# Dividing attention outputs by their sums in twelve pairs instead of eight, with the factors turned in front of the products with V

## The chip, the cores and the metric

The kernel runs on one core of one Trainium2 chip. Its metric is the device time of one execution in microseconds. The engines are TensorE (PE, with weight loads as PEld), VectorE (DVE), ScalarE (ACT), GpSimd (POOL) and SyncE (SP), which only issues transfers. Each works through its own queue in the order in which the program was written to it, and waits where an instruction needs another engine's result or a buffer that is still in use.

## The reference

Attention with a causal window of 128 and four sink columns, then a feed-forward layer with a cosine, then a mixture of experts with one expert a token. The change touches the division by the row sum in the attention.

```python
def _attn_ref(q, k, v, n_sink, window):          # 4 batches, 8 heads, S = 768, D = 64
    scores = scale * np.matmul(q, k.transpose(0, 1, 3, 2))
    keep = is_sink | in_window                    # 4 sink columns, window 128
    scores = np.where(keep, scores, -1000000000.0)
    scores = scores - np.max(scores, axis=-1, keepdims=True)
    a = np.exp(scores)
    a = a / (np.sum(a, axis=-1, keepdims=True) + 1e-09)
    return np.matmul(a, v)
x = attn_out.transpose(0, 2, 1, 3).reshape(3072, 512)
h = x @ w_in                                      # 512 x 2048
x = (h * np.cos(h)) @ w_out                       # 2048 x 512
...
out[mask] = gate_w[mask, None] * (np.maximum(x[mask] @ w1[e], 0.0) @ w2[e])   # 8 experts, top 1
```

Since the division is by one number a row, it can be made on P = exp(scores) before the product with V, or on the product. Everything is kept in float32 by a high part and a rest: a tile named ..._h holds the rounded value and ..._l what it leaves, and a product is formed of three.

## The kernel before

The sequence of a batch is worked on in two halves of 384 rows (three blocks of 128). There are eight such half-sequences, hb 0 to 7, with four pairs of heads each: pairs 0 to 3 are hb 0, pairs 4 to 7 hb 1, pairs 8 to 11 hb 2, and so on to pair 31. While the attention of hb runs, the same program runs the feed-forward layer on tile hb−1, whose products are hp (with w_in) and y (with w_out). In the first third it also converts the weights from their loaded form into high part and rest (cv_in, cv_out, cv_s, cv_a, wi_l, wo_l). The mixture of experts comes last.

The steps of one pair, in the order of the code: q and k are turned on TensorE (pq L447, pk L469) and split; scores ps for each block and head, from which VectorE takes the masked values and their row maxima mx (L548); exp with the row sums sm on ScalarE (L564); P is turned block by block (pt L588, L589) and split into pT_h (ScalarE) and pT_l (VectorE); the sink columns are copied to pc, turned to pz (L613) and split into sp; and the product with V is added up in po. po is the transposed output of two heads, 128 x 384: a column is a row of the sequence.

The division has two forms, chosen by `whole`.

- `whole` (hb 2 and later before the change): P itself is multiplied by 1/sum. For each of the three blocks VectorE adds 1e-9 to two sums and takes the reciprocal (L571), and in hb 2 POOL multiplies the two heads' P (helper line L142, called at L576); from hb 3 on VectorE does. Behind po ScalarE copies it to xT_h (L644) and VectorE subtracts to xT_l (L645, recorded under the helper line L148).
- not `whole` (hb 0 and 1 before): one addition and one reciprocal for all six columns of sm (L598). POOL spreads the factors to 128 columns, one copy a block (L601), TensorE turns these three (pf), ScalarE copies pf to xs (L651), VectorE multiplies po by it (L652), ScalarE rounds to xT_h (L653) and POOL subtracts to xT_l (L654).

From hb 3 on the products with V use another, stacked form; its division is the `whole` one. In hb 0 and 1 the odd pairs are "extra": they have tiles of their own for P (pb_x) and their loads.

All of ps, pt, pz, po, pf, pq and pk come from one rotation of three banks of PSUM (the extra pairs of hb 0 use the three banks of y instead), so a tile has to wait until the one that stood three places earlier in that rotation has been read. A scheduler takes the instructions as the code yields them, with weights for the steps, and sets the order of each engine's queue from its own costs; that order is then fixed.

Of the kernel before, what the change touches and what calls it, by code (L numbers as in the profile page):

```python
# [11 lines left out]
F32 = DT.float32  # L12
# [4 lines left out]
AF = mybir.ActivationFunctionType  # L17
# [3 lines left out]
P = 128  # L21
# [27 lines left out]
EX = 1  # L49
# [5 lines left out]
NPOOL = 3  # L55
# [6 lines left out]
def kernel(  # L62
# [23 lines left out]
    HALF = S // 2  # L86
    NQ = HALF // P
# [14 lines left out]
    PE, ACT, DVE, POOL, SP = nc.tensor, nc.scalar, nc.vector, nc.gpsimd, nc.sync  # L102
# [21 lines left out]
    def ps_a(name):  # L124
        return ps_rot(0, "a", name)
# [4 lines left out]
    def ps_y(i, name):  # L130
        return psum.tile([P, 512], F32, tag=f"y{i}", name=name, bufs=1)
# [3 lines left out]
    def mm(o, l, r, start, stop):  # L135
        PE.matmul(o, l, r, start=start, stop=stop)  # L136
# [14 lines left out]
    ident = const.tile([P, P], F32, name="ident")  # L151
# [76 lines left out]
    pb_x = [wpool.tile([P, DM], F32, name=f"pb_x{f}", tag=f"wi_h{f}") for f in range(NE1, NF)]  # L228
# [6 lines left out]
    apool = att.enter_context(tc.tile_pool(name="apool", bufs=1, side="right"))  # L235
# [84 lines left out]
    def steps(hb):  # L320
        return STEPS_0 if hb <= 1 else STEPS_1
# [82 lines left out]
    def attn_front(hb, pr):  # L404
# [3 lines left out]
        h0 = 2 * pr  # L408
        extra = hb <= EX and pr % 2 == 1

        whole = hb > EX
        n_ps = [0]

        def psb(name):
            if hb > 0 or not extra:
                return ps_a(name)
            n_ps[0] += 1
            return ps_y(n_ps[0] % NQ, name)
# [29 lines left out]
        stack = hb >= STACK  # L448
# [118 lines left out]
        def rest():  # L567
            xh, xl = xT[hb]
            for t in range(NQ if whole else 0):
                ts(DVE, sm[:, 2 * t:2 * t + 2], sm[:, 2 * t:2 * t + 2], 1e-9, ALU.add)  # L570
                DVE.reciprocal(sm[:, 2 * t:2 * t + 2], sm[:, 2 * t:2 * t + 2])  # L571
                for j in range(2):
                    c0, c1, _ = cols(t)
                    i = 2 * t + j
                    if hb < NPOOL:
                        ts(POOL, Pb[t][j][:, c0:c1], Pb[t][j][:, c0:c1], sm[:, i:i + 1], ALU.mult, 0.0, ALU.add)  # L576
                    else:
                        ts(DVE, Pb[t][j][:, c0:c1], Pb[t][j][:, c0:c1], sm[:, i:i + 1], ALU.mult)
            yield steps(hb)[3]
            pT_h = apool.tile([P, 2, NQ * 256], F32R, name="pT_h")  # L580
            pT_l = apool.tile([P, 2, NQ * 256], F32R, name="pT_l")
            for t in range(NQ):
                pt = psb("pt").rearrange("p (j x) -> p j x", j=2)
                first = half == 0 and t == 0
                s0 = P if first else 0
                for j in range(2):
                    if not first:
                        PE.transpose(pt[:, j, 0:P], Pb[t][j][:, 0:P], ident)  # L588
                    PE.transpose(pt[:, j, P:2 * P], Pb[t][j][:, SEG:W3], ident)  # L589
                oh = pT_h[:, :, t * 256 + s0:(t + 1) * 256]  # L590
                ol = pT_l[:, :, t * 256 + s0:(t + 1) * 256]
                ACT.activation(out=oh, in_=pt[:, :, s0:256], func=AF.Copy)
                tt(DVE, ol, pt[:, :, s0:256], oh.bitcast(F32), ALU.subtract)
                yield steps(hb)[4]
            if not whole:

                ts(DVE, sm, sm, 1e-9, ALU.add)
                DVE.reciprocal(sm, sm)  # L598
                rb = [pb_x[t + NQ * (pr % 2)][:, 3 * P:4 * P] for t in range(NQ)]
                for t in range(NQ):  # L600
                    POOL.tensor_copy(rb[t].rearrange("p (j d) -> p j d", d=D),  # L601
                                     sm[:, 2 * t:2 * t + 2].unsqueeze(2).to_broadcast([P, 2, D]))
            t0 = 2 if half == 0 else 0
            pc = apool.tile([P, NQ, 2, NS], F32, name="pc")
            if extra:
                for t in range(t0, NQ):
                    for j in range(2):
                        POOL.tensor_copy(pc[:, t, j], Pb[t][j][:, P:SEG])
            else:
                (POOL if hb < NPOOL else DVE).tensor_copy(pc[:, t0:], Pt[:, t0:, :, P:SEG])  # L610
            pz = psb("pz")
            for t in range(t0, NQ):
                PE.transpose(pz[0:2 * NS, t * P:(t + 1) * P], pc[:, t].rearrange("p j s -> p (j s)"), ident)  # L613
            sh, sl = sp[0:2 * NS], sp[2 * NS:4 * NS]
            if half == 0 and pr == 0:

                POOL.memset(sp[0:4 * NS, 0:t0 * P].bitcast(F32), 0.0)
            ACT.activation(out=sh[:, t0 * P:], in_=pz[0:2 * NS, t0 * P:HALF], func=AF.Copy)
            tt(DVE, sl[:, t0 * P:], pz[0:2 * NS, t0 * P:HALF], sh[:, t0 * P:].bitcast(F32), ALU.subtract)
            yield steps(hb)[5]  # L620
            def band(blk):

                own = blk if half == 0 else blk - 1
                ta, tb = max(own, 0), min(own + 1, NQ - 1)
                c0 = ta * P
                c1 = (tb + 1) * P
                m0 = own * 256 + P if own >= 0 else 0
                return c0, c1, m0, m0 + (c1 - c0)

            if not stack:  # L630

                po = psb("po")
                mm(po[:, 0:HALF], vs[:, 0:2 * D], sp, True, False)
                mm(po[:, 0:HALF], vs[:, 2 * D:4 * D], sp, False, False)
                for j in range(2):
                    for blk in range(nblk):
                        c0, c1, m0, m1 = band(blk)
                        vh, vl = [vp[:, blk, (o + j) * D:(o + j + 2) * D] for o in (0, 3)]
                        mm(po[:, c0:c1], vh, pT_h[:, j, m0:m1], False, False)
                        mm(po[:, c0:c1], vh, pT_l[:, j, m0:m1], False, False)  # L640
                        mm(po[:, c0:c1], vl, pT_h[:, j, m0:m1], False, j == 1 and blk == nblk - 1)
                        yield steps(hb)[6]
                if whole:
                    ACT.activation(out=xh[:, pr, :], in_=po[:, 0:HALF], func=AF.Copy)  # L644
                    tt(DVE, xl[:, pr, :], po[:, 0:HALF], xh[:, pr, :].bitcast(F32), ALU.subtract)  # L645
                else:
                    pf = psb("pf")
                    for t in range(NQ):
                        mm(pf[:, t * P:(t + 1) * P], rb[t], ident, True, True)
                    xs = apool.tile([P, HALF], F32, name="xs")  # L650
                    ACT.activation(out=xs, in_=pf[:, 0:HALF], func=AF.Copy)  # L651
                    tt(DVE, xs, po[:, 0:HALF], xs, ALU.mult)  # L652
                    ACT.activation(out=xh[:, pr, :], in_=xs, func=AF.Copy)  # L653
                    tt(POOL, xl[:, pr, :], xs, xh[:, pr, :].bitcast(F32), ALU.subtract)  # L654
            if stack:
                xs = apool.tile([P, HALF], F32, name="xs")
            for j in range(2 if stack else 0):

                po = psb("po")
                mm(po[:, 0:HALF], vs[:, j * 2 * D:(j + 1) * 2 * D], sp, True, False)  # L660
                for blk in range(nblk):
                    c0, c1, m0, m1 = band(blk)
                    mm(po[:, c0:c1], vp[:, blk, 3 * j * D:(3 * j + 2) * D], pT_h[:, j, m0:m1], False, False)
                    mm(po[:, c0:c1], vp[:, blk, (j + 1) * D:(j + 3) * D], pT_l[:, j, m0:m1], False, blk == nblk - 1)
                    yield steps(hb)[6]
                r = slice(j * D, (j + 1) * D)
                ACT.activation(out=xs[r], in_=po[r, 0:HALF], func=AF.Copy)
                tt(DVE, xs[r], po[(1 - j) * D:(2 - j) * D, 0:HALF], xs[r], ALU.add)
            if stack:
                ACT.activation(out=xh[:, pr, :], in_=xs, func=AF.Copy)  # L670
                tt(POOL, xl[:, pr, :], xs, xh[:, pr, :].bitcast(F32), ALU.subtract)
            for dst, x_ in ((xg_h, xh), (xg_l, xl)):
                SP.dma_start(out=x_[:, pr, :].bitcast(F32), in_=dst[half, b * H + h0:b * H + h0 + 2].rearrange("j d q -> (j d) q"), cond=bad_r > 0, cond_hint=False)
            yield steps(hb)[7]
# [376 lines left out]
    for hb in range(1, NTILE):  # L1051
# [8 lines left out]
        whole = attn_weight(hb) * ATT_STEPS[hb % 2] * (S_FIRST if hb == 1 else 1.0)  # L1060
# [31 lines left out]
    for nm in ("xT_h", "xT_l"):  # L1092
        t = xpool.tile([P, KD, 256], F32R, name="m_" + nm, tag=nm)
# [344 lines left out]
```

## Time and profile before

| | us |
|---|---|
| median of three runs | 1224.01 (1221.92 to 1226.13) |
| profiled execution, its own time | 1220.77 |
| its span | 1218.9 |
| TensorE busy | 1140.5 (94%) |
| VectorE busy | 799.0 (66%) |
| ScalarE busy | 698.7 (57%) |
| POOL busy | 341.0 (28%) |

The mean granted clock of TensorE is 0.974 of full speed over the span; in the second of forty slices of the span it is 0.7, in the third and the sixth 0.8. The share of TensorE grows along the program: 32.47 of the first 50 us, 41.33 of the next, and from 260 us on nearly all. A row of the profile names line, engine and operation, then what is written and read; a wait is given as the idle time in front of an instruction and what ended it.

### The profile page before, as it was taken

To read this page: it belongs to the slowest core of one execution; us is meant where nothing else is said; L and a number is where in the kernel's file an instruction comes from. 1 tells how busy PE (TensorE), PEld (TensorE's weight loads), DVE (VectorE), ACT (ScalarE), POOL (GpSimd) and SP (SyncE) were. 2 spreads that over 40 slices of the span, in tenths; PEclk is the share of its full clock that TensorE was granted. 3 is DMA by queue.
4 is the path that set the end of the run, shared out by engine and by line. 5 is a ranking of instruction groups with operands and counts; after the bars stand their busy time and mean duration, and the time that the engine had idled before them with its cause. 6 is when DMAs were issued, how large, how long until landed. Compare 5 with 4: busy or idle time off the path is not lost. (4 is left out here: it accounts for less than half of the span.)

```text
span 1218.9 us, 21841 instructions
## 1 busy us (share of the span) xinstructions
PE 1140.5 (94%) x6688; PEld 1007.7 (83%) x6688; DVE 799.0 (66%) x2293; ACT 698.7 (57%) x1451; POOL 341.0 (28%) x396
## 2 busy tenths in 40 slices
PE   5888897899999999999999999999999999899995
PEld 4667776788878888988889888999889988789984
DVE  7886798968887888788878878464672223722220
ACT  4667576678767777877688876333422224622221
POOL 2534545542223223322232222231212112112110
PEclk9789989999999999999999999999999999999998
DMA  5553255534332343334224322261424113212110
GB/s 142 138 164 121 84 170 162 163 95 98 81 95 69 84 103 97 82 77 104 77 78 116 96 70 78 92 246 53 104 92 162 37 44 133 88 45 63 37 37 24
DMA packets 141338, 118.87 MB, mean 98 GB/s; under 512 B 98415, under 2 KB 107631, under 8 KB 141168
## 3 DMA queue, kind: packets, MB, share of 16 engines
q1 hardware_dynamic: 136848, 103.29, 30.5%
q0 software_dynamic: 4320, 13.65, 3.5%
q8 instruction: 66, 1.08, 0.4%
q14 instruction: 104, 0.85, 0.2%
HBM read 151.32 MB, written 19.67 MB: 140 GB/s over the span
## 5 line engine op out<-in xcount | busy, mean ns | idle before, releaser
L148 POOL TENSOR_TENSOR g_l<-ch,g_h 128x384 fp32r<-128x384 f32 x128 | 131.8, 1030 | 413.3 <-ACT g_h L760 379.7
L136 PE MATMUL hp<-xT_h,wi_h 128*128 128x384 f32 x512 | 183.1, 358 | 1.5 <-DVE ch L148 1.5
L136 PE MATMUL hp<-xT_l,wi_h 128*128 128x384 f32 x512 | 174.5, 341 | 0.0
L136 PE MATMUL hp<-xT_h,wi_l 128*128 128x384 f32 x512 | 174.2, 340 | 0.0
L688 PE MATMUL y<-wo,g_h 128*128 128x512 f32 x384 | 160.4, 418 | 0.4 <-ACT y_part L778 0.4
L688 PE MATMUL y<-wo_l,g_h 128*128 128x512 f32 x384 | 158.5, 413 | 0.0
L688 PE MATMUL y<-wo,g_l 128*128 128x512 f32 x384 | 156.0, 407 | 0.2 <-POOL g_l L148 0.2
L136 PE MATMUL m_y<-wi_h,hT 128*128 128x512 f32 x416 | 132.7, 394 | 1.6 <-ACT hT L1182 0.7
L145 DVE SCALAR_TENSOR_TENSOR hT<-m_h,hT 128x256 fp32r<-128x256 f32 x88 | 37.4, 425 | 145.5 <-ACTq L1346 97.1
L750 ACT ACTIVATE ch<-ch,cols 128x384 f32<-128x384 f32 x128 | 78.9, 616 | 89.2 <-DVE ch L145 88.0
L136 PEld LDWEIGHTS hp<-xT_h,wi_h 128*128 128x128 f32 x512 | 97.9, 191 | 6.7 <-DVE ch L148 1.8
L136 PEld LDWEIGHTS hp<-xT_l,wi_h 128*128 128x128 f32 x512 | 97.9, 191 | 3.8 <-issue 0.2
L142 DVE TENSOR_SCALAR ch<-hp 128x384 int32<-128x384 f32 x128 | 71.1, 555 | 43.5 <-PE hp L136 26.7
L136 PEld LDWEIGHTS hp<-xT_h,wi_l 128*128 128x128 f32 x512 | 97.2, 190 | 0.4
L136 PEld LDWEIGHTS m_y<-wi_h,hT 128*128 128x128 f32 x416 | 78.0, 188 | 18.7 <-ACT hT L1182 1.5
L760 ACT ACTIVATE g_h<-ch 128x384 fp32r<-128x384 f32 x128 | 66.4, 519 | 42.1 <-DVE ch L148 32.3
L564 ACT ACTIVATE Pb<-Pb,mx 128x272 f32<-128x272 f32 (+1 forms) x168 | 82.7, 493 | 13.5 <-DVE mx L548 12.9
L148 DVE TENSOR_TENSOR ch<-ch,hp 128x384 f32<-128x384 f32 x128 | 70.2, 550 | 27.8 <-ACT ch L750 26.2
L1163 ACT ACTIVATE hT<-m_h 128x256 fp32r<-128x256 f32 x88 | 33.7, 383 | 90.2 <-PE m_h L136 84.4
L688 PEld LDWEIGHTS y<-wo,g_l 128*128 128x128 f32 x384 | 73.6, 192 | 14.3 <-POOL g_l L148 0.6
L1197 POOL DMA_INDIRECT out_dram<-m_ot,m_ids x26 | 26.7, 1027 | 198.5 <-ACT m_ot L1194 147.9
L136 PE MATMUL ps<-kT_hl,qT_h 64*128 64x272 f32 (+3 forms) x264 | 59.0, 348 | 24.2 <-DVE mx L548 10.3
(307 smaller groups left out, 2958.0 us busy)
## 6 DMA issues: line engine op xcount, KB each, us to landing
rw<-in_moe_w_dram SPq DMA_DIRECT2D x112, 512.0 KB
wo_l<-wl_scr SPq DMA_DIRECT2D x122, 256.0 KB
cv_in<-in_moe_w_in_dram SPq DMA_DIRECT2D x16, 512.0 KB
cv_out<-in_moe_w_out_dram SPq DMA_DIRECT2D x16, 512.0 KB
y_scr<-yt SPq DMA_DIRECT2D x24, 256.5 KB
xT_h<-xg_h SPq DMA_DIRECT2D x32, 192.0 KB
xT_l<-xg_l SPq DMA_DIRECT2D x32, 192.0 KB
qn<-in_q_dram SPq DMA_DIRECT2D x56, 96.0 KB
```

Of the source, the lines that this page charges most:

```text
L136: PE.matmul(o, l, r, start=start, stop=stop)
L142: e.tensor_scalar(out=o, in0=i, scalar1=s1, scalar2=s2, op0=op0, op1=op1)
L145: e.scalar_tensor_tensor(out=o, in0=i0, scalar=s, in1=i1, op0=op0, op1=op1)
L148: e.tensor_tensor(out=o, in0=a, in1=b, op=op)
L564: ACT.activation(out=Pb[t][j][:, c0:c1], in_=Pb[t][j][:, c0:c1], func=AF.Exp, scale=-1.0, bias=mx[:, i:i + 1], accum_out=sm[:, i:i + 1])
L688: i = PE.matmul(o, l, r, start=start, stop=stop)
L750: ACT.activation(out=ch, in_=ch, func=AF.Sin, scale=TWO_PI, bias=half_pi)
L760: ACT.activation(out=gh, in_=ch, func=AF.Copy)
L1163: ACT.activation(out=hT_h[f], in_=hp, func=AF.Relu)
L1197: POOL.indirect_dma_start(out=out[:, :], out_offset=bass.IndirectOffsetOnAxis(ap=m_ids[T % 4][:, h:h + 1], axis=0), in_=m_ot[h], in_offset ...
```

## The change

`whole` now begins at hb 3 instead of hb 2, so that pairs 8 to 11 divide the output too. In all twelve pairs the spread factors rb no longer lie in spare columns of pb_x but in the first 128 columns of the first head's P of each block, which the copies may overwrite once TensorE has turned them. The matmuls pf and ScalarE's copy to xs are written in front of pz and po instead of behind po.

```diff
-        whole = hb > EX
+        whole = hb >= NPOOL
...
                 yield steps(hb)[4]
+            xs = None if whole and not stack else apool.tile([P, HALF], F32, name="xs")
             if not whole:
 
                 ts(DVE, sm, sm, 1e-9, ALU.add)
                 DVE.reciprocal(sm, sm)
-                rb = [pb_x[t + NQ * (pr % 2)][:, 3 * P:4 * P] for t in range(NQ)]
+                rb = [Pb[t][0][:, 0:P] for t in range(NQ)]
                 for t in range(NQ):
                     POOL.tensor_copy(rb[t].rearrange("p (j d) -> p j d", d=D),
                                      sm[:, 2 * t:2 * t + 2].unsqueeze(2).to_broadcast([P, 2, D]))
+                pf = psb("pf")
+                for t in range(NQ):
+                    mm(pf[:, t * P:(t + 1) * P], rb[t], ident, True, True)
+                ACT.activation(out=xs, in_=pf[:, 0:HALF], func=AF.Copy)
...
                 else:
-                    pf = psb("pf")
-                    for t in range(NQ):
-                        mm(pf[:, t * P:(t + 1) * P], rb[t], ident, True, True)
-                    xs = apool.tile([P, HALF], F32, name="xs")
-                    ACT.activation(out=xs, in_=pf[:, 0:HALF], func=AF.Copy)
                     tt(DVE, xs, po[:, 0:HALF], xs, ALU.mult)
...
-            if stack:
-                xs = apool.tile([P, HALF], F32, name="xs")
             for j in range(2 if stack else 0):
```

NPOOL is 3 and EX is 1. The scheduler sets new orders from this. On POOL, at pair 8 (the first of hb 2), before:

```order
L142 TENSOR_SCALAR Pb<-Pb,sm 128x128 x2
L148 TENSOR_TENSOR g_l<-ch,g_h 128x384
L142 TENSOR_SCALAR Pb<-Pb,sm 128x272 x4
L610 COPY pc<-Pb 128x32
L148 TENSOR_TENSOR g_l<-ch,g_h 128x384
L148 TENSOR_TENSOR wi_l_2093<-cv_a,wi_h_2087 128x512
```

and after, where g_l is the rest of a feed-forward tile and wi_l that of a weight:

```order
L148 TENSOR_TENSOR g_l<-ch,g_h 128x384
L615 COPY pc<-Pb 128x32
L602 COPY Pb<-sm 128x128 x2
L148 TENSOR_TENSOR g_l<-ch,g_h 128x384
L602 COPY Pb<-sm 128x128
L148 TENSOR_TENSOR wi_l_2093<-cv_a,wi_h_2087 128x512
```

The six multiplications are gone, and of the three copies of the factors the last stands behind a g_l.

On TensorE, at the last transposes of pair 11 after the change:

```order
L588 MATMUL pt<-ident,Pb 128x128
L589 MATMUL pt<-ident,Pb 128x128
L136 MATMUL pf<-ident,Pb 128x128 x3
L686 MATMUL y_2354<-wo_121,g_h 128x512
L686 MATMUL y_2354<-wo_l,g_h 128x512
L618 MATMUL pz<-ident,pc 32x128
```

The three pf follow the last transpose of P directly; before there were none in this pair.

On VectorE, at the end of pair 7, before:

```order
L142 TENSOR_SCALAR cv_a<-cv_out 128x512
L145 SCALAR_TENSOR_TENSOR cv_a<-cv_out,cv_a 128x512
L142 TENSOR_SCALAR ch<-hp 128x384
L145 SCALAR_TENSOR_TENSOR cv_a<-cv_out,cv_a 128x512
L145 SCALAR_TENSOR_TENSOR ch<-hp,ch 128x384
L145 SCALAR_TENSOR_TENSOR cv_a<-cv_s,cv_a 128x512
L148 TENSOR_TENSOR xs<-po,xs 128x384
L148 TENSOR_TENSOR ch<-ch,hp 128x384
```

and after:

```order
L142 TENSOR_SCALAR cv_a<-cv_out 128x512
L142 TENSOR_SCALAR ch<-hp 128x384
L145 SCALAR_TENSOR_TENSOR cv_a<-cv_out,cv_a 128x512
L145 SCALAR_TENSOR_TENSOR ch<-hp,ch 128x384
L148 TENSOR_TENSOR xs<-po,xs 128x384
L145 SCALAR_TENSOR_TENSOR cv_a<-cv_out,cv_a 128x512
L148 TENSOR_TENSOR ch<-ch,hp 128x384
L145 SCALAR_TENSOR_TENSOR cv_a<-cv_s,cv_a 128x512
```

xs, the product of the output with its factors, has moved in front of two conversion steps (cv_a).

## Rows read from the trace of the kernel before

**Rows 1.** Busy time by stretch: us of each engine, PEclk, DMA share, GB/s

```profile
155.00:260.00 105.00, 94.22 (x502) 78.56 (x501) 93.04 (x215) 76.40 (x157) 55.63 (x65) 0.91 0.55 158
260.00:310.00 50.00, 49.77 (x298) 44.63 (x297) 38.31 (x106) 40.32 (x79) 14.08 (x16) 1.00 0.35 84
```

**Rows 2.** TensorE's waits, 0 to 155 us: total us, times, longest

```profile
PE pt L588 <- DVE xs L148: 3.0, 1, 3.0
PE pk L469 <- DVE xs L148: 2.9, 1, 2.9
```

**Rows 3.** The same view, 155 to 262 us

```profile
PE ps L136 <- DVE mx L548: 5.7, 3, 2.6
PE ps L136 <- DVE xT_l L148: 4.5, 3, 2.4
```

**Rows 4.** Groups, 20 to 262 us: xcount | busy us, mean ns | idle

```profile
L148 POOL TENSOR_TENSOR xT_l<-xs,xT_h 128x384 fp32r<-128x384 f32 x8 | 8.2, 1022 | 11.3 <-ACT xT_h L653 11.3
...
L136 PE MATMUL pf<-ident,pb_x 128*128 128x128 f32 x48 | 7.6, 288 | 0.7 <-DVE kT_hl L148 0.7
L601 POOL COPY pb_x<-sm 128x128 f32<-128x128 f32 x24 | 7.4, 345 | 13.7 <-DVE sm L598 13.7
...
L651 ACT ACTIVATE xs<-pf 128x384 f32<-128x384 f32 x8 | 3.9, 484 | 1.4 <-PE pf L136 1.4
...
L140 DVE TENSOR_SCALAR sm<-sm 128x2 f32<-128x2 f32 x12 | 2.7, 237 | 0.4 <-ACT Pb L564 0.4
...
L571 DVE RECIPROCAL sm<-sm 128x2 f32<-128x2 f32 x12 | 1.7, 156 | 0.1
...
L598 DVE RECIPROCAL sm<-sm 128x6 f32<-128x6 f32 x8 | 1.5, 183 | 0.0
...
L140 DVE TENSOR_SCALAR sm<-sm 128x6 f32<-128x6 f32 x8 | 1.3, 163 | 0.0
```

**Rows 5.** Timeline, 143.5 to 152.5 us: start, us, engine, operation [idle]

```profile
144.19 0.88 PE L136 MATMUL pf<-ident,pb_x 128*128 128x128 f32 x6
...
149.21 0.68 DVE L145 SCALAR_TENSOR_TENSOR cv_a<-cv_out,cv_a 128x512 int32<-128x512 int32 x1
149.81 0.55 DVE L145 SCALAR_TENSOR_TENSOR ch<-hp,ch 128x384 f32<-128x384 f32 x1
...
150.28 0.68 DVE L145 SCALAR_TENSOR_TENSOR cv_a<-cv_s,cv_a 128x512 f32<-128x512 f32 x1
...
150.88 0.55 DVE L148 TENSOR_TENSOR xs<-po,xs 128x384 f32<-128x384 f32 x1
...
151.48 0.55 PE L469 MATMUL pk<-ident,kn 128*128 128x128 f32 x3 [2.94 <-DVE xs L148]
```

**Rows 6.** Timeline 164 to 172 us, VectorE and POOL

```profile
165.74 1.00 POOL L148 TENSOR_TENSOR g_l<-ch,g_h 128x384 fp32r<-128x384 f32 x1
165.76 1.52 DVE L145 SCALAR_TENSOR_TENSOR cv_a<-cv_in,cv_a 128x512 int32<-128x512 int32 x1
...
167.75 0.68 DVE L145 SCALAR_TENSOR_TENSOR cv_a<-cv_in,cv_a 128x512 int32<-128x512 int32 x1
```

**Rows 7.** Timeline, ps behind xT_l in pairs 8 to 10

```profile
183.57 0.39 PE L136 MATMUL ps<-kT_hl,qT_h 64*128 64x272 f32 x1 [0.64 <-DVE xT_l L148]
...
213.44 0.72 PE L136 MATMUL ps<-kT_hl,qT_h 64*128 64x272 f32 x4 [2.42 <-DVE xT_l L148]
...
238.93 0.39 PE L136 MATMUL ps<-kT_hl,qT_h 64*128 64x272 f32 x1 [1.44 <-DVE xT_l L148]
```

**Rows 8.** Timeline 189 to 193 us, TensorE

```profile
189.67 0.52 PE L136 MATMUL ps<-kT_hl,qT_h 64*128 64x272 f32 x3 [2.57 <-DVE mx L548]
...
192.83 0.52 PE L136 MATMUL hp<-xT_h,wi_h 128*128 128x384 f32 x1
```

**Rows 9.** Timeline 263 to 268 us, behind pair 11

```profile
263.05 0.47 ACT L644 ACTIVATE xT_h<-po 128x384 fp32r<-128x384 f32 x1
...
267.84 0.34 PE L136 MATMUL hp<-xT_h,wi_h 128*128 128x384 f32 x1
```


## The prediction

> **What bounds the kernel now.** I read the table of busy time by stretch first, to see which engine has no room where the change works. From 155 to 260 us, where hb 2 (pairs 8 to 11) runs, TensorE is busy for 94.2 of 105 us and VectorE for 93.0; the granted clock is 0.91, a mix of the 1.2 and 2.4 GHz levels. From 260 us TensorE is busy for 49.77 of 50 us at clock 1.00 [rows 1]. So whatever the change does to the time, it does before 260 us, where TensorE still has gaps; later only added or removed TensorE work counts, and pairs 12 to 31 keep theirs.
>
> Then the table of waits, for what TensorE stands still for. In pairs 0 to 7 two waits for xs (the product of the output with its factor) cost 3.0 and 2.9 us [rows 2]. In hb 2 it waits 5.7 us for mx, the row maxima, and 4.5 us, three times, for xT_l, the rounding rest of the output [rows 3]. All of these are VectorE results. The timeline shows the kind of wait. Pair 7's po must be read by xs before its bank can be used again; xs starts only at 150.88, right behind weight-conversion steps (cv_a) at 149.21 and 150.28, and TensorE's pk, which needs the bank, starts at 151.48 after 2.94 us [rows 5]. So it is the place of xs in VectorE's queue, more than the work of the pair, that is late. No wait of pf (the transposed factors) for its POOL copies is in the groups: its idle time is 0.7 us in all, put down to VectorE [rows 4]. Those copies are done long before they are needed.
>
> **The change, part by part.** Everything is worked out against the profiled execution, 1220.77 us, span 1218.9; it lies 3.2 us under the median of the three runs, 1224.01, so I add the sum to the median.
>
> *A, more work on TensorE in hb 2.* Each of the four pairs gains three matmuls, six records. In the trace six records take 0.88 us [rows 5], of which the last one's 0.29 [rows 4] is mostly pipeline, so one starts each (0.88 − 0.29)/5 = 0.12 us and a pair costs 0.7 us, 2.8 us for four. The half-clock level doubles that to 5.7 us: hp takes 0.52 us at 192.83 behind a wait of 2.57 us and 0.34 us at 267.84 [rows 8, 9]. What may hide it: ps of the next pair waits for xT_l by 0.64, 2.42 and 1.44 us [rows 7], and when VectorE's queue sets that moment, a later TensorE only waits less. Pairs 9 and 10 are then hidden, pair 8 but for 0.06, and pair 11, with no such wait behind it, pays 0.7. I take +0.8, between 0 and +5.7.
>
> *B, a new wait of pf for its copies.* The factors now go into columns of P, so each copy must wait until TensorE has transposed that block, and pf stands in front of pz and po. What is queued behind a waiting pf is everything TensorE has: the pair's pz and po and the FFN products. Before, copies went into spare columns early. The trace has no such wait, so I bound it: 0 if other work lies between the last transpose and pf; at most three copies of 0.345 us [rows 4] in all twelve pairs, 12 × 1.0 = +12 us. By the new order pair 11 has nothing in between, while two copies are still to run behind a g_l: 2 × 0.345 = 0.7 us. In pairs 2, 6 and 8 the third copy stands behind a two-input POOL operation (g_l takes 1.0 us [rows 6]), with three y matmuls or a few hp to cover it: about 0.4 us each, an estimate. Elsewhere I see cover. Sum 0.7 + 3 × 0.4 = +1.9.
>
> *C, VectorE in hb 2.* Out go twelve small sums and twelve reciprocals, 2.7 + 1.7 = 4.4 us; in come four of each on six columns, 4 × (0.163 + 0.183) = 1.4 us [rows 4]. The multiplication xs, 0.55 us [rows 5], takes the place of the subtraction xT_l of as many elements. So VectorE has 3.0 us less, in the stage in which it is late. The whole gain reaches TensorE only if those operations stand in front of a result it waits for; many stand in gaps. I take −1.0, bounds −3.0 and 0.
>
> Against this stands a slowdown that the timeline shows. A cv_a step takes 1.52 us at 165.76, beside POOL's g_l of 165.74, and 0.68 us at 167.75, with POOL still [rows 6]. The change gives POOL one two-input subtraction of 1.02 us [rows 4] in each of four pairs, where VectorE subtracted before; each can cost a conversion step 0.84 us, 3.4 in all, which puts the upper bound of C at +0.4. The Trainium skill, page "GPSIMD Engine Reference", section "Key points", says that GpSimd shares its SBUF interfaces with VectorE and contends with VectorE instructions in a two-port mode or with two SBUF inputs. The two rows agree: both are cv_a steps with two SBUF inputs. By that rule alone C would come out at +0.4 rather than −1.0, and the sum below at +1.9.
>
> *D, pairs 0 to 7: pf and its copy to xs moved ahead of po.* Nothing is added. po's bank is now followed by other tiles, so at 151.48 pk takes pz's bank and no longer waits for xs; the next ps does. In VectorE's new order xs stands two conversion steps earlier, 0.6 us each by the distance of starts from 149.21 to 149.81 and from 150.28 to 150.88 [rows 5]. I take −1.2: the bound below is −2.9, all of the wait, and above 0, since ps also needs kT_hl, which VectorE makes behind the same steps. The other wait, 3.0 us of pt in pair 7, stays: the third transposed block waits instead of the second, and xs stands behind the same number of conversions.
>
> *E, the rest, taken at nothing.* ScalarE gets one more copy of 0.484 us [rows 4] a pair, 2.0 us; it is busy for 76.4 of 105 us there [rows 1], and hidden as long as the copy isn't queued ahead of pT_h or the sp that po waits for; uncovered, +2.0. POOL loses 24 multiplications and gains twelve copies and four subtractions; it isn't waited for except in B. xT_l of pair 11 becomes longer (product, copy, POOL subtraction), but tile 2 begins its first product at 267.84 while xT_h of pair 11 was copied at 263.05 [rows 9]; about a microsecond more fits.
>
> Sum: +0.8 + 1.9 − 1.0 − 1.2 = +0.5 us, so 1224.0 + 0.5 = 1224.5.
>
> **Rivals.** *The banks come free earlier and TensorE's waits for VectorE go.* For it: po is now read by one operation instead of a ScalarE copy and then a VectorE subtraction, and 2.9 + 4.5 us of waits are for exactly this release [rows 2, 3]. Against it: the subtraction stands in the same queue in which conversions made pair 7's xs late [rows 5], and multiplying instead of subtracting does not move those. If it happens, −2.9 − 4.5 − 1.5 (half of C) + 0.8 + 1.9 = −6.2: 1217.8 us.
>
> *pf waits in most pairs.* This is the slower one: TensorE, in order, stands at pf until POOL has made the third copy. For it: the copies now sit between a transpose and a matmul of the same pair, in a queue with operations of 1.0 us, and in pair 11 with nothing between. Against it: TensorE would have waited for VectorE a little later anyway in many pairs, and there the two waits merge. With 0.7 us a pair, 12 × 0.7 = 8.4 in place of 1.9, the sum is +7.0: 1231.0 us. It decides from about 0.5 us a pair that is not given back.
>
> *The waits only change their names.* pk no longer waits for xs but ps waits for kT_hl; the time VectorE saves in hb 2 falls into its own gaps; pf's work and waits are covered by the waits behind them. C, D, A and B are all about 0: 1224.0 us. This is the case in which the change does not do what it says, as far as time goes.
>
> **How the numbers follow.** A measurement of this kernel tells about 0.3%, 3.7 us, from no change. I give my forecast 0.30 and the case of changed names 0.13; both lie within 3.7 us. Free banks get 0.29 and waiting pf 0.28. So faster 0.29, same 0.43, slower 0.28. For the range I go from a little under the gain of the free banks to a little over the price of the waiting pf, 1216 to 1232; all lower bounds together (−3.0 − 2.9 = −5.9) lie inside, all upper ones together (+20) would not, but B's +12 needs every pair uncovered. The likeliest case alone has 1221 to 1228.
>
> **What would show it.** A: 24 more pf records between 165 and 260 us, and shorter waits for what replaces xT_l in pairs 8 to 10. B: pf in the table of waits, released by POOL, about 2 us in four pairs; over 6 us proves the slower rival. C: VectorE's busy time from 155 to 260 us lower by some 3 us; cv_a steps beside POOL's new subtractions at 1.5 us would show that it is given back. D: no wait of pk for xs, and xs of pair 7 some 1.2 us earlier; if ps then waits for kT_hl, the time is kept. If the wait for the release of po in hb 2 vanishes altogether, my reading that VectorE's queue sets it is wrong. Any difference that arises after 260 us would be outside the argument.

## The result and the profile after

The changed kernel takes 1235.8 us (median of four runs, 1234.92 to 1240.74) against 1222.97 for the kernel before (median of four); the ratio is 1.0114, interval 1.0096 to 1.0132, that is 11.7 to 16.1 us more. The forecast was 1224.5 with a range up to 1232: slower than the whole range. The profiled execution has 1235.28 us and a span of 1233.3, 14.4 us more than the profiled one of before.

Where the time is lost shows in the starts of ScalarE's rounding xT_h, which every pair has once. These are pairs 3, 7, 12 and 31, first before and then in the changed kernel (start in us, duration, engine, line, operation):

```profile
80.53 0.52 ACT L653 ACTIVATE xT_h<-xs 128x384 fp32r<-128x384 f32 x1
...
152.09 0.52 ACT L653 ACTIVATE xT_h<-xs 128x384 fp32r<-128x384 f32 x1
...
292.21 0.51 ACT L670 ACTIVATE xT_h<-xs 128x384 fp32r<-128x384 f32 x1
...
760.79 0.53 ACT L670 ACTIVATE xT_h<-xs 128x384 fp32r<-128x384 f32 x1
```

```profile
84.93 0.52 ACT L653 ACTIVATE xT_h<-xs 128x384 fp32r<-128x384 f32 x1 [0.49 <-DVE xs L148]
...
151.58 0.51 ACT L653 ACTIVATE xT_h<-xs 128x384 fp32r<-128x384 f32 x1
...
299.35 0.51 ACT L668 ACTIVATE xT_h<-xs 128x384 fp32r<-128x384 f32 x1
...
767.84 0.53 ACT L668 ACTIVATE xT_h<-xs 128x384 fp32r<-128x384 f32 x1
```

So in these two traces the kernel is 4.4 us late at pair 3, level at pair 7 (−0.5), 7.1 us late at pair 12, and stays so to the end of the attention (+7.05 at pair 31). The span is 14.4 us longer: half of the loss comes behind pair 31, in the mixture of experts, whose code the change does not touch.

The first half, in the table of busy time by stretch [rows 1 for before]:

```profile
155.00:260.00 105.00, 93.37 (x489) 78.77 (x489) 85.66 (x191) 75.46 (x155) 50.06 (x54) 0.89 0.50 151
260.00:310.00 50.00, 48.72 (x292) 44.12 (x293) 36.70 (x103) 38.69 (x78) 15.26 (x19) 1.00 0.36 92
```

VectorE has 85.7 us to do in this window instead of 93.0 (work is also shifted along the time axis by the delay), TensorE is as busy as it was, and its granted clock is 0.89 instead of 0.91. The waits of TensorE, from 0 to 155 us [rows 2]:

```profile
PE ps L136 <- DVE xs L148: 4.1, 2, 3.1
PE pf L136 <- DVE pT_l L148: 2.8, 3, 2.4
...
PE pt L588 <- DVE xs L148: 0.6, 1, 0.6
...
PE pf L136 <- POOL Pb L602: 0.5, 1, 0.5
```

and from 155 to 262 us [rows 3]:

```profile
PE ps L136 <- DVE mx L548: 7.5, 5, 3.7
PE ps L136 <- ACT kT_hl L486: 1.8, 1, 1.8
PE ps L136 <- DVE xs L148: 1.2, 2, 0.6
PE pt L588 <- DVE qT_l L148: 1.2, 1, 1.2
PE hp L136 <- DVE ch L148: 1.1, 1, 1.1
PE ps L136 <- DVE kT_hl L490: 0.8, 1, 0.8
PE ps L136 <- DVE kT_hl L148: 0.2, 1, 0.2
```

Of the two waits of 3 us for xs in [rows 2], that of pk is gone and that of pt is 0.6. But ps now waits 4.1 us for xs, at 41.74 and 56.05, in hb 0, where it waited 0.2 before: the waits for xs are 4.7 us in all instead of 6.1. From 155 us on, the 4.5 us of [rows 3] behind the release of po have become 1.2 (xs). But mx rose from 5.7 to 7.5, and waits for kT_hl, qT_l and ch stand where hardly any stood: in this stretch 13.8 us in all instead of 10.8 (with 0.6 in two small ones; a wait of 1.0 us for kT_hl, at 153.82 before, lies just ahead of this window). The groups by form, 20 to 272 us (count, busy us, mean ns, idle before it) [rows 4]:

```profile
L602 POOL COPY Pb<-sm 128x128 f32<-128x128 f32 x24 | 8.3, 354 | 20.3 <-PE pt L588 10.6 <-DVE sm L599 8.8 <-DMA kn<-in_k_dram 0.6
...
L136 PE MATMUL pf<-ident,Pb 128*128 128x128 f32 x48 | 7.3, 286 | 0.8 <-POOL Pb L602 0.5 <-DVE pT_l L148 0.3
...
L136 PE MATMUL pf<-ident,pb_x 128*128 128x128 f32 x24 | 5.4, 361 | 2.6 <-DVE pT_l L148 2.6
...
L140 DVE TENSOR_SCALAR sm<-sm 128x6 f32<-128x6 f32 x12 | 2.5, 208 | 0.0
...
L599 DVE RECIPROCAL sm<-sm 128x6 f32<-128x6 f32 x12 | 2.2, 182 | 0.1
```

72 records of pf instead of 48, and the wait of pf for POOL's copies is 0.5 us in all.

The second half stands in the timeline of TensorE. The last product of one tile of the experts (m_y) is followed by a jump over code that this tile does not need, and by the first product of the next (m_h). Before:

```profile
1030.76 0.39 PE L136 MATMUL m_y<-wi_h,hT 128*128 128x512 f32 x1
1030.98 0.39 PE L136 MATMUL m_h<-wi_h,m_xT_h 128*128 128x512 f32 x1
...
1034.94 0.50 PE L136 MATMUL m_h<-wi_h,m_xT_h 128*128 128x512 f32 x1 [0.40 <-issue]
```

The products go on without a gap for fifteen matmuls; the sixteenth starts 0.40 us late, "issue", the profile's word for a wait for nothing that it shows. After, the same place and one near the end:

```profile
1038.42 0.39 PE L136 MATMUL m_y<-wi_h,hT 128*128 128x512 f32 x1
...
1043.48 0.77 PE L136 MATMUL m_h<-wi_h,m_xT_h 128*128 128x512 f32 x1 [4.67 <-issue]
...
1208.27 0.47 PE L136 MATMUL m_h<-wi_h,m_x 128*128 128x512 f32 x1 [2.15 <-issue]
```

TensorE stands for 4.67 us at the jump itself, and again for 2.15 us at 1208, where before there were 0.46 and 0.21, eleven and twelve products behind that jump.

### The profile page after: what moved, and what is told of

Same layout as the page of the kernel before. It is cut to its first block, busy times and chain, and to the rows that moved or that the text cites. A ratio compares the mean times of both kernels' runs of the same rounds, so it can differ in the third digit from the quotient of the medians.

```text
span 1233.3 us, 21865 instructions
## 1 busy us (share of the span) xinstructions
PE 1147.2 (93%) x6712; PEld 1014.7 (82%) x6712; DVE 793.5 (64%) x2277; ACT 704.2 (57%) x1457; POOL 341.0 (28%) x388
## 3 DMA queue, kind: packets, MB, share of 16 engines
q8 instruction: 66, 1.08, 0.4%
## 4 chain that ended last, share of the span: by engine, by line
PE 42%; issue 14%; DMA 10%; DVE 10%; ACT 4%; POOL 2%; POOLq 1%; DVEq 0%; SPq 0%; ACTq 0%
PE y L686 16%; PE hp L136 15%; DMA out_dram<-m_ot,m_ids 10%; PE po L136 3%; PE ps L136 2%; POOL m_yg L1138 1%; ACT Pb L564 1%; PE pt L588 1%; DVE pT_l L148 1%; PE pl L814 1%; PE yT L803 1%; PE pt L589 1%; DVE ch L142 1%; PE mh L136 1%; ACT L748 1%
## 5 line engine op out<-in xcount | busy, mean ns | idle before, releaser
L686 PEld LDWEIGHTS y<-wo,g_l 128*128 128x128 f32 x384 | 73.0, 190 | 14.2 <-POOL g_l L148 0.8
```

Source lines behind the costliest of these rows:

```text
L686: i = PE.matmul(o, l, r, start=start, stop=stop)
```

## The experiments

Medians are compared with those of the kernel before on the same chip; a ratio has its 95% interval. The last column is the wait at the jump of the experts, and before how many of the m_h products behind it were done.

| run | us | before | ratio | wait at the jump, us (matmuls ahead of it) |
|---|---|---|---|---|
| the change | 1235.8 | 1222.97 | 1.0114 (1.0096 to 1.0132) | 4.67 (0) |
| e1_front_only | 1227.39 | 1219.45 | 1.0070 (1.0043 to 1.0097) | 1.47 (14) |
| e2_hb2_behind_po | 1232.11 | 1219.45 | 1.0093 (1.0068 to 1.0119) | 4.90 (0) |
| e3_pz_thrice | 1229.7 | 1219.45 | 1.0078 (1.0054 to 1.0103) | 4.95 (0) |
| e4_no_pf_hb2 | 1247.35 | 1219.45 | not comparable, see there | 0.39 (15) |
| a1_pz_hb2 | 1233.07 | 1221.39 | 1.0085 (1.0056 to 1.0114) | 4.96 (0) |
| s24_pz_twice | 1227.75 | 1221.39 | 1.0046 (1.0028 to 1.0065) | 3.33 (5) |
| f0_front_hb0 | 1227.89 | 1221.39 | 1.0056 (1.0036 to 1.0076) | 1.48 (14) |
| f1_front_hb1 | 1222.6 | 1221.39 | 1.0018 (0.9998 to 1.0038) | 0.48 (16) |
| s256_pz | 1235.77 (one run) | 1222.38 | | 0.94 (15) |
| g1_front_spare | 1228.6 | 1222.38 | 1.0047 (1.0026 to 1.0067) | 2.31 (14) |

A single trace is a rough guide to the attention: three kernels that are the same up to hb 7 (e3, s24, s256) stood +0.6, +4.9 and +2.0 us at pair 12 in their traces. What rests on the attention is therefore taken from medians where it can be. Behind pair 31 the traces agree better: from pair 31's rounding to the end of the span it is 464.6 to 467.2 us in the four traces with 48 added TensorE instructions, 463.4 with 24, and 456.6 to 461.0 in the six with none or with 256 (e4 is left out).

**More TensorE instructions and nothing else.** The transposes to pz write the same values again:

```diff
             for t in range(t0, NQ):
-                PE.transpose(pz[0:2 * NS, t * P:(t + 1) * P], ..., ident)
+                for _ in range(3 if hb == NTILE - 1 else 1):       # e3
+                    PE.transpose(pz[0:2 * NS, t * P:(t + 1) * P], ..., ident)
# s24: 2 if hb == NTILE - 1 else 1
# a1:  7 if hb == 2 else 1                     (one transpose a pair there)
# s256: 1 + 10 + 2 * (pr == 3) + (pr == 2 and t < 2) if hb == NTILE - 1 else 1
```

> The kernel before with the three transposes to pz of each pair of hb 7 made three times over: 24 more matmuls and 24 more weight loads on TensorE, as many as the change adds, and nothing else. Theory, the place of TensorE's instructions in the blocks in which they are fetched decides the 'issue' waits: 24 x 0.11 = 2.6 us in hb 7 and some 6 us in the mixture of experts, 1230 to 1233 us. Rival, those waits have another cause (the later start, transfers): 2.6 us alone, 1225 to 1227.

e3 is 9.5 us slower (1.0078), at the expected 8.6 within its interval, and its products in hb 7 cannot cost more than a few us: at pair 31 its trace stands +2.67, at the end +9.2. The wait at the jump is back, at the same instruction as in the changed kernel:

```profile
1038.68 0.77 PE L136 MATMUL m_h<-wi_h,m_xT_h 128*128 128x512 f32 x1 [4.95 <-issue]
```

So 48 TensorE instructions added ahead bring the second half of the loss; the division has nothing to do with it. Nor has the later start: e1 and f0 are 11.0 and 8.5 us late at pair 31 and wait 1.5 us there.

> The kernel before with the transposes to pz of hb 7 made twice: 12 matmuls and 12 weight loads more, half as many as in the run with three. Theory, the wait for 'issue' depends on where the code of the branch lies in the blocks that are fetched: it is either there with about its whole length (4 to 5 us) or nearly not at all (under 1.5 us). Rival, it grows with the number of instructions: about half, 2.5 us. Time 1221 to 1222 without and 1226 with it.

The wait is 3.33 us, between the rival's 2.5 and the theory's 4 to 5, and the time, 1227.75, is above what both expected. It is not a share of the same wait: it has moved. This is TensorE in s24, from the first m_h behind the jump:

```profile
1036.11 0.39 PE L136 MATMUL m_h<-wi_h,m_xT_h 128*128 128x512 f32 x1
...
1037.02 0.39 PE L136 MATMUL m_h<-wi_l,m_xT_h 128*128 128x512 f32 x1
1040.74 0.79 PE L136 MATMUL m_h<-wi_h,m_xT_l 128*128 128x512 f32 x1 [3.33 <-issue]
```

With no added instruction fifteen matmuls are done before the wait, with 24 (twelve matmuls and twelve weight loads) five, with 48 none. The boundary moves forward by about as many instructions as were added in front. The next code arrives a nearly fixed time after the jump (3.96 us behind the first m_h before, 4.63 in s24, 5.64 at the longest, in g1), and the matmuls that still lie in front of the boundary cover a part of it.

> The kernel before with 128 more transposes to pz in hb 7: 128 matmuls and 128 weight loads, 256 TensorE instructions. TensorE's code is fetched in packets of 16,384 bytes; if an instruction takes 64 bytes, 256 of them shift the code by exactly one packet. Theory: the boundary lies at the same place behind the jump as in the kernel before, so the wait for 'issue' near 1030 to 1060 us is 0.3 to 1.6 us and stands some 15 matmuls behind the jump; the time is that of before plus 128 x 0.11 = 14 us, 1234 to 1238. Rival, any added code brings the wait at the jump: 4.5 to 5 us there, and 1239 or more.

```profile
1045.78 0.39 PE L136 MATMUL m_h<-wi_h,m_xT_h 128*128 128x512 f32 x1
...
1048.95 0.39 PE L136 MATMUL m_h<-wi_h,m_xT_l 128*128 128x512 f32 x1
1050.29 0.50 PE L136 MATMUL m_h<-wi_h,m_xT_h 128*128 128x512 f32 x1 [0.94 <-ACT wi_h L1107]
```

With 256 instructions the boundary is back where it was: fifteen matmuls ahead, and 0.94 us of wait, which the profile puts down to ScalarE. The trace is +14.7 us at pair 31 and +15.0 at the end, so the experts cost nothing more; the other jump has its two short waits again, 0.47 and 0.19 us. That fits a block of 256 instructions, one packet of the queue q8, from which TensorE's code comes. The page of the changed kernel has 66 of them with 1.08 MB, 16.4 KB each, and that of s256, the second line, one more:

```profile
q8 instruction: 66, 1.08, 0.4%
...
q8 instruction: 67, 1.10, 0.4%
```

That q8 brings TensorE's code the traces show in two more ways. From 200 to 900 us of the trace before it has 31 packets for 3962 matmuls and 3960 weight loads, 256 a packet. And in all twelve traces the wait at the jump ends 1.2 to 1.6 us after a packet of q8 has come in.

The Trainium skill, page "Runtime: NRT & Kernel Launch", section "Instruction fetch mechanics", says of this: instruction memory is refilled in blocks of 16 KiB, which are 256 instructions, and a taken branch whose target is not held forces a fetch before execution goes on. The traces agree in the size of the block (256 matmuls and weight loads a packet) and give the price here, up to 4.96 us a jump.

> The kernel before with the transpose to pz in each of hb 2's four pairs made seven times over: 24 more matmuls and 24 weight loads, 0.7 us a pair, at the place where the changed kernel has its pf, and nothing else. The prediction's step A says that most of it is hidden by waits for VectorE: about +0.8 us at pair 12. The theory now, after the changed kernel, says that it costs its time in full: +2.8 us at pair 12. Both expect a wait for 'issue' of 4.5 to 5 us at about 1040 us in the mixture of experts, since TensorE has 48 instructions more: 1226 to 1230 in all.

a1 puts the 48 instructions into hb 2, where TensorE has gaps. It is 10.4 us slower (6.8 to 13.9), e3 with as many in hb 7, where it has next to none, 9.5 (6.6 to 12.6). The time, 1233.07, is above the expected 1230. The added work costs about the same at both places, but the difference of the two is known to some 4.5 us only, so whether waits hide 2 us of it in hb 2 is not shown. Its trace stands +8.2 at pair 12, 5.4 more than 2.8, which is a little beyond the scatter told above.

**The changed kernel without one part.**

```diff
-        whole = hb >= NPOOL
+        whole = hb > EX                        # e1: hb 2 as before
# e2: the kernel before, with
-        whole = hb > EX
+        whole = hb >= NPOOL
+                rb = [(pb_x[t + NQ * (pr % 2)][:, 3 * P:4 * P] if hb <= EX else Pb[t][0][:, 0:P]) for t in range(NQ)]
```

> The changed kernel with hb 2 given back its old form (P divided by POOL before the transposes); only pairs 0 to 7 keep the new place of pf and of the factors in P. TensorE has as many instructions as before the change. Theory: the move of pf in eight pairs is worth about -0.5 us at pair 7, as the changed kernel's trace shows there, and the long waits for 'issue' in the mixture of experts (4.7 and 2.2 us in the changed kernel) come from the 48 added TensorE instructions: here 1221 to 1225 us, and no such wait over 1 us. Rival, the move of pf or another queue's shift causes them: they stay, and the time is 1228 or more.

It is 7.9 us slower by medians, and no case that was written down: the wait at the jump is small (1.47, where the theory had at most 1), but the move of pf in eight pairs, which should have gained 0.5, costs most of this. In its trace hb 2, whose code is that of before, has these waits of TensorE, 155 to 275 us:

```profile
PE ps L136 <- DVE xT_l L148: 7.9, 3, 3.5
PE ps L136 <- ACT kT_hl L486: 4.0, 1, 4.0
```

kT_hl stood at 1.0 before (at 153.82) and xT_l at 4.5 [rows 3]; in e3, s24 and s256, unchanged there too, they have 0.9 to 1.0 and 4.5 to 5.3. Only mx fell, from 5.7 to 1.8. Work whose code was not changed waits longer, in queues that the scheduler put in another order.

> The kernel before with hb 2's pairs in the new form, pf still behind po in all twelve pairs; hb 2's factors lie in P. TensorE has the same 48 instructions more as the changed kernel. Theory: the added matmuls cost their 2.8 us and something for the wait of the bank, at most 5 us by pair 12, and the waits for 'issue' in the mixture of experts appear (about 6 us): 1230 to 1234 us. Rival, the loss lies in pf standing in front of pz and po: at most 3 us by pair 12, and without the waits for 'issue' 1224 to 1226.

As the theory said, 1232.1: 12.7 us by medians (8.3 to 14.5 by the ratio), with the wait of 4.90 at the jump; at pair 12 its trace stands +7.5, above the 5 that the theory allowed. The total is what 48 instructions cost in a1 and e3, give or take 4 us: the new form of division in hb 2 has no measurable gain or loss of its own beside its added matmuls.

```diff
-                pf = psb("pf")
...
+                if hb > EX:                    # e4
+                    ACT.activation(out=xs.rearrange("p (t c) -> p t c", c=P), in_=ident.unsqueeze(1).to_broadcast([P, NQ, P]), func=AF.Copy)
+                else:
+                    pf = psb("pf")
...
```

> The changed kernel without the three pf matmuls in hb 2's four pairs: ScalarE fills xs from the identity instead (so those pairs are multiplied by wrong factors), all else stays. TensorE has as many instructions as before the change. Theory: no 'issue' wait over 1 us in the mixture of experts, and 2.8 us less in hb 2: 1225 to 1228 us. Rival, the matmuls were hidden and the loss in hb 2 is one of order: by pair 12 the same 7 us as the changed kernel, 1229 to 1231 without the 'issue' waits and 1235 with them.

Its total says nothing, since with other factors other experts are chosen and the tiles of the experts take other paths. What can be read lies ahead of that. At pair 12 it stands +5.0 us instead of +7.1, 2.1 less without the matmuls. These are single traces, but they are within 0.1 us of each other at pair 7, and how the 2.1 comes about bears on step A: from 152 us to pair 12 TensorE waits 17.3 us in e4 against 13.8 in the changed kernel, for mx above all (9.5 against 7.5), at a granted clock of 0.94 against 0.92. So waits took the place of the matmuls, and the 2.1 us go with the clock. At the jump it has the kernel before's picture to a hundredth, fifteen matmuls, then 0.39 us. Taking the instructions out takes the wait out.

**The move of pf alone, by half.**

```diff
-                rb = [pb_x[t + NQ * (pr % 2)][:, 3 * P:4 * P] for t in range(NQ)]
+                rb = [(Pb[t][0][:, 0:P] if hb == 0 else pb_x[t + NQ * (pr % 2)][:, 3 * P:4 * P]) for t in range(NQ)]
...
+                if hb == 0:                    # f0; f1: hb == 1; then not behind po
+                    xs = apool.tile([P, HALF], F32, name="xs")
+                    pf = psb("pf")
...
# g1: e1 with
-                rb = [Pb[t][0][:, 0:P] for t in range(NQ)]
+                rb = [pb_x[t + NQ * (pr % 2)][:, 3 * P:4 * P] for t in range(NQ)]
```

> The kernel before with factors in P and pf in front of pz and po in pairs 0 to 3 alone. TensorE does the same work in another order. Theory: the move lets pf wait in hb 0 (the changed kernel was 4.4 us late at pair 3 and had made it good by pair 7), and what is left at pair 12 comes from how the queues fall out: late by 3 to 6 us at pair 3, anything from -1 to +6 at pair 12, 1219 to 1226 in all. Rival, the move costs a fixed price a pair: half of the +10.7 us at pair 12 that the move in eight pairs had, 1224 to 1226.

> The same move in pairs 4 to 7 alone. Theory: no loss in pairs 4 to 7 (the changed kernel gained there), and at pair 12 what the queues' new order in hb 2 brings, whose code is unchanged: between -1 and +8 us. If it is 4 us or more, the loss in hb 2 comes from the order and not from the new form of division. Rival, a fixed price a pair: half of +10.7 at pair 12, most of it in pairs 4 to 7.

> The kernel with pf moved in front of pz and po in pairs 0 to 7 only, but with the factors left in the spare columns of pb_x, so that the copies need not wait for the transposes of P. TensorE's order is that of the run with the move in eight pairs and factors in P (8.5 us slower than before). Theory: the factors' place costs nothing and the place of pf, with the order and the banks that follow from it, costs all: again 6 to 10 us, 1226 to 1231. Rival, the wait for the copies behind the transposes is the price: within 3 us of before, 1219 to 1224.

The move costs 6.8 us in pairs 0 to 3 (4.4 to 9.3), 2.2 in pairs 4 to 7 (−0.2 to 4.6), and 8.5 in both (5.2 to 11.8): the halves add up. f0 is above both of its cases, which end at 1226. The trace of f1 stands −0.9 us at pair 7 and +7.0 at pair 12, more than the 4 us that were to show a loss in hb 2 by order alone; but the profiled execution was 3.2 us slower than f1's median, so this is not shown. The price is in hb 0, where f0's trace is 6.4 us late at pair 3. All five traces with the move in hb 0 stand +4.3 to +7.4 there, the seven without it 0 to +3.6. In hb 0 ps of the next pair now waits for xs, since po is the last tile of a pair, and pt for mx. TensorE's waits in f0, 20 to 92 us:

```profile
PE ps L136 <- DVE xs L148: 2.7, 1, 2.7
PE pt L588 <- DVE mx L548: 1.7, 2, 1.0
```

Before, that wait for xs was 0.2 us there. The waits in this stretch add up to about as much as before (11.5 us against 11.3). Nor does the granted clock explain it. This is the stretch from 20 to 90 us before, in f0 and in the changed kernel, where it is 0.83, 0.80 and 0.86:

```profile
20.00:90.00 70.00, 58.62 (x313) 48.80 (x311) 59.21 (x155) 46.75 (x128) 28.34 (x43) 0.83 0.55 150
```

```profile
20.00:90.00 70.00, 58.02 (x294) 48.21 (x295) 55.25 (x147) 43.97 (x123) 29.59 (x43) 0.80 0.50 133
```

```profile
20.00:90.00 70.00, 56.63 (x303) 47.15 (x303) 56.71 (x152) 45.50 (x128) 31.39 (x43) 0.86 0.53 140
```

The changed kernel is late at pair 3 at a higher clock than before, and the six other traces with an unchanged hb 0 have 0.80 to 0.86. What makes up the loss in hb 0 is open. With the factors in their old place (g1) the move costs 5.7 us (3.2 to 8.2): that much is the place of pf. The 2.8 us between this and e1's 8.5, for factors that wait for the transposes of P, are less than the noise of the two.

No version tried beats the kernel before.

## Why the prediction was wrong

**The opening step.** "Whatever the change does to the time, it does before 260 us" failed. It was right that TensorE's work from pair 12 on stays the same and false that its time then must. In the traces 6.6 of the 14.4 us come from the two jumps in the experts: the kernel is 7.7 us late ahead of the first and 13.2 behind it, and 14.2 behind the second (waits of 4.67 instead of 0.40 and of 2.15 instead of 0.67, and time at half clock, where a product takes 0.77 us instead of 0.39). e3 brings this without the change, s256 takes it away again. The prediction named "any difference that arises after 260 us" as outside the argument, and there it arose. Without the jumps the changed kernel would be at about 1229 us, an estimate (1235.8 − 6.6), inside the range and still some 5 us above the forecast; that rest is of the parts below.

**A** is not settled between +0.8 and the full +2.8. The waits for xT_l, which were to hide it, did go (4.5 to 1.2), but waits for other VectorE results took their place. e3 against a1, a stage without gaps against one with, is too coarse for 2 us; in e4 the waits grew by 3.5 us when the matmuls went, which speaks for some hiding. The rows given for the doubling at half clock (0.52 against 0.34 us) show a factor of 1.5; the product behind the jump (0.77 against 0.39) shows two.

**B** was too high and its rival wrong: pf waits 0.5 us for POOL, not 1.9, and not 8.4. pf waits for VectorE's pT_l instead (2.8 us in pairs 0 to 7), as pz had done. In f1 pf does wait 3.2 us for POOL, at 122.87 and 130.45, so this wait hangs on the order. The slower result is not the slower rival's.

**C**: VectorE lost its small operations (12 + 12 on six columns remain, 2.5 + 2.2 us), and this bought nothing that shows: mx went from 5.7 to 7.5 us. The contention with POOL hardly came about either: of the four new subtractions, at 189.96, 219.94, 248.48 and 272.56 us, only the first ran beside a cv_a step for more than 0.1 us, and that step took 1.06 us instead of 0.68, half of it beside a wi_l. e2 against a1 has room for −1.0 as for +0.4; they are not told apart.

**D** had the wrong sign: −1.2 was forecast for the move, and alone it costs 8.5 us (e1, 5.2 to 11.8). It was worked out at pair 7, but the price is mostly in hb 0 (6.8 us in f0, 2.2 in f1), where ps now waits for xs (4.1 us instead of 0.2), and how those waits become the whole price is open. At pair 7 pk no longer waits, as predicted, and the wait of pt, which was to stay, fell from 3.0 to 0.6; but xs came at 150.94 instead of 150.88, not 1.2 us earlier, and behind it the order on ScalarE is worse for the next scores. The timeline of the changed kernel at pair 8:

```profile
150.94 0.54 DVE L148 TENSOR_TENSOR xs<-po,xs 128x384 f32<-128x384 f32 x1
...
153.89 0.63 ACT L306 ACTIVATE wo<-cv_a 128x512 fp32r<-128x512 f32 x1 [0.44 <-DVE cv_a L145]
...
154.43 0.66 ACT L272 ACTIVATE cv_s<-cv_in 128x512 f32<-128x512 f32 x1
...
154.98 0.48 ACT L486 ACTIVATE kT_hl<-pk 128x384 fp32r<-128x384 f32 x1
...
155.51 0.33 PE L136 MATMUL ps<-kT_hl,qT_h 64*128 64x128 f32 x2 [1.82 <-ACT kT_hl L486]
```

kT_hl, which the next scores need, stands behind wo and cv_s, a weight conversion that itself waits for VectorE; before it was copied at 153.29, behind qT_h, and ps waited 1.0 us. Across e1, g1 and f0 the move has 5.7 to 8.5 us. They wait 1.5 to 2.3 us at the jump, but only in g1 is the stretch behind pair 31 longer than before (by 2.9 us; e1 has 0.0, f0 −1.5). In the changed kernel, with hb 2 changed as well, about 12.8 − 6.6 − 2.8 = 3.4 us are left for it, if A costs its full 2.8: the prices do not add (e1 and e2 together would be 20), and why the two orders together cost less than one is open.

**E**: the tail of pair 11 held, and ScalarE's copy was not tried alone. From pair 12 to pair 31 the distance stays at 7.1 us.

The rival of free banks was half right in its mechanism (−2.9 and −3.3 us of those waits) and wrong in its result: ps waits 3.9 us more for xs in hb 0, and in hb 2 other VectorE results were late by as much.

## What to carry to other kernels

Before an edit that adds or removes instructions on a busy engine, look behind its jumps: where code is skipped, the wait depends on where the target lies in the 256-instruction blocks, and a change of 48 instructions far ahead can cost 5 us there. A wait that a change removes from an engine in order is gained only if the next thing it needs is ready; count the waits of the whole stretch, not the one that goes. And where a scheduler sets the order, compare a variant with one that has the same instructions and does nothing, as e3 here, before a loss is put down to the idea.

## What the runs showed that was not expected

The wait at one and the same jump in TensorE's code: 0.4 to 2.3 us with no instruction added in front, 3.33 with 24, 4.67 to 4.96 with 48, and 0.94 with 256; code arrives 4.0 to 5.6 us after the jump, 1.2 to 1.6 us before TensorE goes on a packet of its queue has come in. Unchanged code in hb 2 waited 7.9 us for xT_l and 4.0 for kT_hl (e1) where it had waited 4.5 and 1.0, with no change but the order of the queues. And moving the three small matmuls of pf ahead of the work that needs them, with no instruction added, cost 4.4 to 9.3 us in four pairs.
